# Two attention decodes on one core: the last 64 rows of A's wq moved in two 32-partition transfers

## The chip, the cores and the metric

The kernel runs on one core of one Trainium2 chip. The metric is the device time of one execution in microseconds. Before the change the median of three runs is 248.11 us (248.06 to 248.28).

## The reference

Two independent decode steps, A and B, each project one token, attend over a cache and project back. The outputs of both stand side by side. All arrays are bfloat16.

```python
# shapes of both: x [1,1,576], k_cache and v_cache [1,16,8192,128], wq [576,4096], wo [4096,576]
# 32 query heads of 128, 16 key/value heads, two query heads on each
q = (x @ wq).reshape(B, Sq, Hq, Dh)
k, v = ...            # A: the last W = 2048 positions of the cache; B: all 8192
scores = einsum(q, k) * Dh ** -0.5
o = einsum(softmax(scores), v)
out = o.reshape(B, Sq, Hq * Dh) @ wo
...
concatenate([a, b], axis=-1)   # [1,1,1152]
```

With one token the work is nearly all reading: per side 4.5 MB of wq and 4.5 MB of wo, for A 16 MB of cache, for B 64 MB, 102.8 MB in all.

## The kernel before

Every engine has a list of operations, written in program order by `op` and `load` (class `Prog`, L37 to L109); a wait is put ahead of an operation for each name in its `deps`. SP issues all big loads, one after another; ACT issues the two small loads of x.

**The ring.** All big loads go into one SBUF buffer, `ring`, of 73728 bfloat16 columns on 128 partitions. `place` (L181) takes the next stretch of columns (going back to the beginning where the rest is too short), lets the load wait for the last use of whatever lay there, and appends it to SP's list. The order of loads is: A's wq, B's wq, then K0, K1, V0, K2, V1, ... over twelve units (four of A with four key heads each, eight of B with two), then A's wo in one piece and B's wo in six pieces of 16, 8, 4, 2, 1 and 1 blocks of 576 columns.

**wq.** The 576 rows of a wq are loaded in two transfers. The main one (L212) puts rows 0 to 511 on 128 partitions, four consecutive rows on each. The tail (L214) takes the last 64 rows; each row of 4096 columns is cut into two halves, so that 64 rows become 128 partitions of 2048 columns: row r has its first half on partition 2r and its second on 2r + 1.

**The query projection.** The x row is spread over partitions by PE: `xT` (L282) multiplies pieces of x by a row of ones, which gives x values as columns, each repeated 128 times; DVE copies them into `xrep`. For the tail, `xdup` (L273) holds each of the last 64 values twice, and two copies with a mask (L288) make one version that is zero on odd partitions and one that is zero on even ones, so that the product with the halves of a row picks the right half. Then `qmm` (L323) makes, for each side, eight groups of 512 columns, with five matmuls each: four with main rows and one with the tail. A `qmm` waits for both wq transfers of its side. Its result goes to `ktb` and from there into `za` (A) and `zb` (B), the stationary operands of the scores.

**Attention.** Per unit, DVE transposes each slab of K (`T`, L367), PE makes the scores (`S`, L384), then come the maximum, the exponential (ACT, L433), another DVE transpose and the products with V (L460), accumulated and folded into one column per head (L476). The loads of later units wait for the `T` and `V` operations that use the ring's stretch before them; the first V loads wait for `qmm0.7` and `qmm1.7`.

**The end.** After the last unit the heads are normalised and multiplied by wo (`F`, L543), first A's piece, then B's six as they land; the 1x576 results of each side are copied to `outsb` (L551, L554) and stored (L555).

Of the kernel before, what the change touches and what calls it, by code (L numbers as in the profile page):

```python
# [14 lines left out]
DM = 576  # L15
# [21 lines left out]
class Prog:  # L37
# [9 lines left out]
    def op(self, eng, fn, deps=(), name=None):  # L47
        self.ops[eng].append((fn, tuple(deps), name, None))
        if name is not None:
            assert name not in self.where, name  # L50
            self.where[name] = (eng, len(self.ops[eng]) - 1)

    def load(self, eng, fn, sem, value, deps=(), name=None):
        self.ops[eng].append((fn, tuple(deps), None, sem))
        if name is not None:
            assert name not in self.dma, name
            self.dma[name] = (sem, value)
# [54 lines left out]
def bass_concat_heads__sliding_block_cached__gqa_block_cached__decode_kernel(nc, A_x, A_k_cache, A_v_cache, A_wq, A_wo,  # L112
                         B_x, B_k_cache, B_v_cache, B_wq, B_wo, out):
    xs, ks, vs = [A_x, B_x], [A_k_cache, B_k_cache], [A_v_cache, B_v_cache]
    wqs, wos = [A_wq, B_wq], [A_wo, B_wo]
# [10 lines left out]
    onesb = nc.alloc_sbuf_tensor("onesb", [1, 128], BF16)  # L126
    xrow = nc.alloc_sbuf_tensor("xrow", [1, 2 * DM], BF16)
    xdup = nc.alloc_sbuf_tensor("xdup", [1, 2, 128], BF16)
    xrep = nc.alloc_sbuf_tensor("xrep", [128, 2, 6, 128], BF16)
# [39 lines left out]
    def view(t, free, offset, dims, parts=128, p0=0):  # L169
        return bass.AP(tensor=t, offset=p0 * free + offset, ap=[[free, parts], *dims])  # L170

    pg = Prog(nc)
    op, load = pg.op, pg.load
    s_x = [nc.alloc_semaphore("s_x%d" % i) for i in range(2)]
    s_ld = [nc.alloc_semaphore("s_ld%d" % i) for i in range(NSEM)]
    s_out = nc.alloc_semaphore("s_out")


# [2 lines left out]
    def place(size, uses, issue, name):  # L181
        if at[0] + size > RING:
            at[0] = 0
        lo, hi = at[0], at[0] + size
        at[0] = hi
        deps = []
        for r in list(live):
            if r[0] < hi and lo < r[1]:
                deps += r[2]
                live.remove(r)  # L190
        n = nload[0]
        nload[0] += 1
        if n >= NSEM:
            deps += uses_of[n - NSEM]
        uses_of.append(list(uses))
        live.append((lo, hi, list(uses)))
        t = ring[:, lo:hi]
        load("sp", lambda e: issue(e, t), s_ld[n % NSEM], 16 * (n // NSEM + 1), deps=deps, name=name)
        return t

    for P in range(2):
        x = xs[P]
# [4 lines left out]
    wq_at = {}  # L207
    w = HQ * DH
    for P in range(2):
        uses = ["qmm%d.7" % P]  # L210
        main = wqs[P][0:512, :].rearrange("(p k) n -> p (k n)", k=4)
        wq_at[P, 0] = place(4 * w, uses, lambda e, t, main=main: e.dma_start(t, main), "wq%d.0" % P)  # L212
        tail = wqs[P][512:DM, :].rearrange("r (c n) -> (r c) n", c=2)
        wq_at[P, 1] = place(w // 2, uses, lambda e, t, tail=tail: e.dma_start(t, tail), "wq%d.1" % P)  # L214


    kv_at = {}
# [17 lines left out]
    for i in range(NU + 1):  # L235
        for kind, n in (("K", i), ("V", i - 1)):
            if 0 <= n < NU:
                side, u = UNITS[n]
# [11 lines left out]
    def slab(kind, side, u, s):  # L250
# [7 lines left out]
       deps=["id0"], name="ident")  # L258
# [7 lines left out]
    for c in range(2):  # L266
        op("dve", lambda e, c=c: e.tensor_reduce(par[:, c:c + 1], view(identf, 128, c, [[2, 64]]), AX.X, ALU.add),
           deps=["identf"], name="par%d" % c)


    banks = [sb[0], sb[1], qb[0], qb[1]]
    for P in range(2):
        op("dve", lambda e, P=P: e.tensor_copy(  # L273
            view(xdup, 256, 128 * P, [[2, 64], [1, 2]], parts=1),
            view(xrow, 2 * DM, P * DM + 512, [[1, 64], [0, 2]], parts=1)), deps=["x%d" % P], name="xd%d" % P)
        for k in range(5):
            def mm(e, P=P, k=k):
                if k < 4:
                    lhsT = view(xrow, 2 * DM, P * DM + k, [[4, 128]], parts=1)
                else:  # L280
                    lhsT = xdup[0:1, P, :]
                return e.matmul(banks[2 * P + k // 4][:, (k % 4) * 128:(k % 4 + 1) * 128], lhsT=lhsT,  # L282
                                rhs=onesb[0:1, :], start=True, stop=True)
            op("pe", mm, deps=["x%d" % P, "onesb", "xd%d" % P], name="xT%d.%d" % (P, k))
        op("dve", lambda e, P=P: e.tensor_copy(
            xrep[:, P, 0:4, :].rearrange("p k m -> p (k m)"), banks[2 * P][:, :]), deps=["xT%d.3" % P], name="xr%d.0" % P)
        for c in range(2):
            op("dve", lambda e, P=P, c=c: e.tensor_scalar(  # L288
                xrep[:, P, 4 + c, :], banks[2 * P + 1][:, 0:128], par[:, c:c + 1], None, ALU.mult),
                deps=["xT%d.4" % P, "par%d" % c], name="xr%d.%d" % (P, 1 + c))  # L290
# [5 lines left out]
    for h in range(2):  # L296
        op("dve", lambda e, h=h: e.tensor_reduce(
            cls[:, 2 * h:2 * h + 2], view(identf, 128, 64 * h, [[1, 2], [32, 2], [2, NB]]), AX.XY, ALU.add),
            deps=["identf"], name="clsB%d" % h)
    op("dve", lambda e: e.tensor_reduce(clsa[:], view(identf, 128, 0, [[1, 8], [8, 16]]), AX.X, ALU.add),  # L300
       deps=["identf"], name="clsa")
    op("dve", lambda e: e.tensor_reduce(sel[:], view(identf, 128, 0, [[1, 32], [32, 4]]), AX.X, ALU.add),
       deps=["identf"], name="sel")
    op("dve", lambda e: e.tensor_copy(mkr[:], view(ident, 128, 0, [[0, 128], [1, 4]], 4)),
       deps=["ident"], name="mkr")
    op("dve", lambda e: e.tensor_scalar(mkl[:], view(ident, 128, 0, [[0, 16], [1, 4], [0, 2]], 4), -1.0, BIG,
                                        ALU.add, ALU.mult), deps=["ident"], name="mkl")

    XR = ["xr%d.%d" % (P, c) for P in range(2) for c in range(3)]

    KT = NKT * SLAB
    for P in range(2):
        for n in range(8):
            u = 8 * P + n
            bank = banks[u % 4]

            def mm(e, P=P, n=n, bank=bank):
                for k in range(5):
                    if k < 4:
                        lhsT, o = xrep[:, P, k, :], wq_at[P, 0][:, k * w + n * 512:k * w + (n + 1) * 512]  # L320
                    else:
                        lhsT, o = xrep[:, P, 4 + n // 4, :], wq_at[P, 1][:, (n % 4) * 512:(n % 4 + 1) * 512]
                    ins = e.matmul(bank[:, :], lhsT=lhsT, rhs=o, start=(k == 0), stop=(k == 4))  # L323
                return ins
            op("pe", mm, deps=["wq%d.0" % P, "wq%d.1" % P] + XR + (["qe%d" % (u - 4)] if u >= 4 else []),
               name="qmm%d.%d" % (P, n))
            deps = ["qmm%d.%d" % (P, n)] + (["qT%d" % (u - 2)] if u >= 2 else [])
            if n % 2 == 0:
                op("act", lambda e, n=n, bank=bank: e.activation(qsb[:, n % 2, :], bank[:, :], ACT.Copy),  # L329
                   deps=deps, name="qe%d" % u)  # L330
            else:
                op("dve", lambda e, n=n, bank=bank: e.tensor_copy(qsb[:, n % 2, :], bank[:, :]),
                   deps=deps, name="qe%d" % u)
            op("dve", lambda e, n=n: e.transpose(  # L334
                ktb[:, n * 512:(n + 1) * 512].bitcast(I32), qsb[:, n % 2, :].bitcast(I32)),
                deps=["qe%d" % u] + (["z0.%d" % i for i in range(4)] if P else []), name="qT%d" % u)
        srcs = [[512, NP], [64, 2], [1, 2], [128, 2]]
        for b in range(4):
            if P == 1:
                op("dve", lambda e, b=b: e.tensor_copy(  # L340
                    view(zb, NP * 4 * ZW, 32 * b + W0, [[4 * ZW, NP], [2 * ZW, 2], [ZW, 2], [1, 2]], 32, 32 * b),
                    view(ktb, KT, b // 2 * 256, srcs, 32, 32 * b)),
                    deps=["qT%d" % u for u in range(8, 16)] + ["zb0"], name="z1.%d" % b)
            else:
                op("dve", lambda e, b=b: e.tensor_copy(
                    view(za, NQ * 4 * ZA, ZA - 128 + 32 * b, [[4 * ZA, NQ], [2 * ZA, 2], [ZA, 2], [1, 8]], 32, 32 * b),
                    view(ktb, KT, 0, [[1024, NQ], [64, 2], [1, 2], [128, 8]], 32, 32 * b)),
                    deps=["qT%d" % u for u in range(8)] + ["za0"], name="z0.%d" % b)
# [135 lines left out]
    for i in range(NU):  # L484
        n = nslab[i + 1] if i + 1 < NU else 0
# [37 lines left out]
       deps=["lsel", "lselA", "nb%d" % last, "mr%d" % last], name="L")  # L523
# [3 lines left out]
        deps=["rl", "O%d" % last], name="on")  # L527
    op("dve", lambda e: e.transpose(oq[:].rearrange("p c k -> p (c k)"), on[:].rearrange("p c k -> p (c k)")),
       deps=["on"], name="oq")
# [6 lines left out]
    for P in range(2):  # L536
        k0 = 0
        for c, kk in enumerate(NWO[P]):
# [11 lines left out]
        r = 64 * P  # L550
        op("act", lambda e, r=r: e.activation(outsb[r:r + 1, :], fb[r:r + 1, 0:288], ACT.Copy),  # L551
           deps=[done], name="f%d.0" % P)
        r = 64 * P + 32
# [37 lines left out]
```

## Time and profile before

| | |
|---|---|
| median of the runs | 248.11 us |
| profiled execution, its time | 248.34 us |
| profiled execution, span of the core's instructions | 246.5 us |
| PE busy | 182.0 us (74%) |
| DVE busy | 146.0 us (59%) |
| ACT busy | 23.6 us (10%) |
| moved by DMA | 102.91 MB, mean 418 GB/s |
| granted TensorE clock, mean | 0.827 |

The span runs from the first instruction of the program to the last; the profiled execution's own time has 1.8 us around it. Times in the views are counted from the span's start. The page's first rows give the busy share of each engine in forty slices of 6.2 us, a digit for each; "DMA" there is the mean of the core's sixteen DMA engines. A DMA has three times: when the queue (SPq) issues it, when its packets run on the DMA engines, and when it lands, which is when the last of its increments reaches the semaphore. The chain that ended last follows the work back from the last instruction: at each step to what released it. The packet records of the trace list, for each packet, its start, its length, its size and its queue; the landing records list every increment of each transfer. Neither names the DMA engine; a packet is put to an engine by its start, 3 ns ahead of the end of the packet before it.

### The profile page before, as it was taken

The page shows a single profiled execution, that of the slowest core. Times are in us where ns is not written, and L with a number is a line of the kernel's source. Part 1 is how long each engine was busy: PE and PEld are TensorE (multiplying, and loading weights), DVE is VectorE, ACT ScalarE, POOL GpSimd, SP SyncE. Part 2 cuts the span into 40 slices and gives each one's busy share as a digit, 9 for nine tenths or more (in the row PEclk, how much of TensorE's full clock was granted, in tenths as well). Part 3 has the DMA queues.
Part 4 walks back from the last instruction along what each step waited for, and adds up shares of the span by engine and source line. Part 5 has one row for each costly group of instructions (what it writes and reads, how often), then busy time and mean ns, then how long its engine had stood idle before and what let it go on. Part 6 is the DMA issues. An engine that isn't in the chain of part 4 may idle for free.

```text
span 246.5 us, 2421 instructions
## 1 busy us (share of the span) xinstructions
PE 182.0 (74%) x1009; PEld 75.6 (31%) x1009; DVE 146.0 (59%) x224; ACT 23.6 (10%) x48; POOL 1.8 (1%) x12
## 2 busy tenths in 40 slices
PE   1169958778868599489769858949929949985694
PEld 0024423223332152152142233224205205231461
DVE  3466976786869569169349448547646836922200
ACT  2002210101201010010001001001001001001000
POOL 2000000000000000000000000000000000000000
PEclk9999997799999958957955976965985895796579
DMA  6999999999999999999999999999999999999992
GB/s 261 425 479 402 433 425 419 425 425 463 431 417 431 425 425 431 423 441 452 441 431 433 425 431 425 425 423 427 431 425 431 449 431 431 431 437 431 401 406 103
DMA packets 5062, 102.91 MB, mean 418 GB/s; under 512 B 566, under 2 KB 828, under 8 KB 1340
## 3 DMA queue, kind: packets, MB, share of 16 engines
q1 hardware_dynamic: 5048, 102.77, 97.6%
q8 instruction: 8, 0.13, 0.2%
q14 instruction: 2, 0.02, 0.0%
q10 hardware_dynamic: 4, 0.00, 0.0%
HBM read 102.76 MB, written 0.00 MB: 417 GB/s over the span
## 4 chain that ended last, share of the span: by engine, by line
DMA 56%; PE 20%; DVE 19%; issue 1%; SPq 1%; ACT 0%; DVEq 0%
DMA ring<-in_B_k_cache_dram 41%; DVE ktb L367 15%; DMA ring<-in_B_wo_dram 10%; DMA ring<-in_A_wq_dram 5%; PE sb L323 4%; PE sb L384 4%; PE qb L384 4%; PE qb L323 3%; PE ob L476 3%; DVE pts L445 2%; PE mb L424 1%; SPq L246 1%; DVE pta L441 0%; PE qb L376 0%; DVE nb L430 0%
## 5 line engine op out<-in xcount | busy, mean ns | idle before, releaser
L367 DVE STREAM_TRANSPOSE ktb<-ring 128x1024 int32<-128x1024 int32 x80 | 95.1, 1221 | 16.7 <-DMA ring<-in_B_k_cache_dram 15.8
L384 PE MATMUL sb<-ktb,zb 128*128 128x512 bf16 x256 | 84.4, 468 | 27.3 <-DVE ktb L367 27.3
L384 PEld LDWEIGHTS sb<-ktb,zb 128*128 128x128 bf16 x256 | 23.2, 109 | 77.6 <-DVE ktb L367 45.3
L460 PE MATMUL vb<-ring,pts 128*16 128x512 bf16 x256 | 20.6, 412 | 2.6 <-DVE pts L445 2.6
L384 PE MATMUL qb<-ktb,za 128*128 128x512 bf16 x64 | 19.1, 436 | 2.9 <-DVE ktb L367 2.9
L476 PEld LDWEIGHTS ob<-sel,xo 128*128 128x128 f32 x96 | 19.5, 285 | 4.9 <-issue 2.2
L399 DVE TENSOR_REDUCE mx<-sb 128x1 f32<-128x512 f32 x8 | 5.5, 692 | 21.9 <-PE sb L384 21.9
L476 PE MATMUL ob<-sel,xo 128*128 128x4 f32 (+1 forms) x96 | 17.7, 309 | 0.7 <-ACT xo L467 0.7
L467 ACT ACTIVATE xo<-vb 128x512 f32<-128x512 f32 x12 | 7.2, 597 | 89.2 <-PE vb L460 89.2
L323 PE MATMUL sb<-ring,xrep 128*128 128x512 bf16 x40 | 11.4, 441 | 5.3 <-DMA ring<-in_A_wq_dram 5.3
L430 DVE COPY nb<-mb 128x1 f32<-128x1 f32 x12 | 1.9, 159 | 21.1 <-PE mb L424 21.1
L433 ACT ACTIVATE psb<-sb,nb 128x512 bf16<-128x512 f32 x8 | 5.5, 687 | 65.3 <-DVE nb L430 65.3
L445 DVE STREAM_TRANSPOSE pts<-psb 64x512 bf16<-64x512 bf16 x16 | 11.0, 688 | 1.0 <-ACT psb L433 0.8
L543 PE MATMUL qb<-ring,oP 128*1 128x288 bf16 x128 | 10.3, 328 | 1.2 <-DMA ring<-in_B_wo_dram 0.6
L384 PEld LDWEIGHTS qb<-ktb,za 128*128 128x128 bf16 x64 | 5.7, 106 | 13.4 <-DVE ktb L367 6.4
L401 PE MATMUL mb<-identf,mx 128*1 128x128 f32 x24 | 4.6, 271 | 7.1 <-DVE mx L399 7.1
L334 DVE STREAM_TRANSPOSE ktb<-qsb 128x256 int32<-128x256 int32 x16 | 7.1, 446 | 4.4 <-ACT qsb L329 4.0
L323 PE MATMUL qb<-ring,xrep 128*128 128x512 bf16 x40 | 9.4, 381 | 0.0
L460 PEld LDWEIGHTS vb<-ring,pts 128*16 128x16 bf16 x256 | 4.1, 90 | 16.9 <-issue 15.6
L323 PEld LDWEIGHTS sb<-ring,xrep 128*128 128x128 bf16 x40 | 4.2, 109 | 11.6 <-issue 8.2
L543 PEld LDWEIGHTS qb<-ring,oP 128*1 128x1 bf16 x128 | 5.6, 94 | 5.8 <-DMA ring<-in_B_wo_dram 2.2
L554 DVE CAST outsb<-qb 1x288 bf16<-1x288 f32 x2 | 0.9, 458 | 10.8 <-PE qb L543 10.8
(73 smaller groups left out, 71.9 us busy)
## 6 DMA issues: line engine op xcount, KB each, us to landing
ring<-in_B_k_cache_dram SPq DMA_DIRECT2D x8, 4096.0 KB, 25.3
ring<-in_B_v_cache_dram SPq DMA_DIRECT2D x8, 4096.0 KB, 33.0
ring<-in_A_k_cache_dram SPq DMA_DIRECT2D x4, 2048.0 KB, 30.9
ring<-in_A_v_cache_dram SPq DMA_DIRECT2D x4, 2048.0 KB, 26.4
ring<-in_A_wo_dram SPq DMA_DIRECT2D x1, 4608.0 KB, 16.4
ring<-in_A_wq_dram SPq DMA_DIRECT2D x1, 4096.0 KB, 12.1
ring<-in_B_wq_dram SPq DMA_DIRECT2D x1, 4096.0 KB, 22.2
ring<-in_B_wo_dram SPq DMA_DIRECT2D x1, 2304.0 KB, 21.5
```

Of the source, the lines that this page charges most:

```text
L323: ins = e.matmul(bank[:, :], lhsT=lhsT, rhs=o, start=(k == 0), stop=(k == 4))
L334: op("dve", lambda e, n=n: e.transpose(ktb[:, n * 512:(n + 1) * 512].bitcast(I32), qsb[:, n % 2, :].bitcast(I32)), deps=["qe%d" % u] + ([" ...
L367: op("dve", lambda e: e.transpose(kt.bitcast(I32), src.bitcast(I32)), deps=["K%d" % i] + (["S%d" % (k - NKT)] if k >= NKT else Z), name="T ...
L384: ins = e.matmul(bank[:, :], lhsT=lhsT, rhs=view(ktb, KT, (k % NKT) * SLAB + 64 * c + v, [[128, 16], [2, 32]]), start=(side == "B" and s = ...
L399: op("dve", lambda e: e.tensor_reduce(mx[:, 0:1], sbank[i][:, :], AX.X, ALU.max), deps=["S%d" % (k0[i] + nslab[i] - 1)] + (["mT%d" % (i - ...
L401: op("pe", lambda e: e.matmul(mb[0:1, 0:128], lhsT=mx[:, 0:1], rhs=identf[:, :], start=True, stop=True), deps=["max%d" % i] + was, name="m ...
L433: op("act", lambda e: e.activation(psb[:, :], sbank[i][:, :], ACT.Exp, bias=nb[:, c:c + 1], scale=SCALE, accum_out=acc), deps=["nb%d" % i, ...
L445: op("dve", lambda e, h=h: e.transpose(view(pts, 1024, 2 * h, [[4, 16], [64, 16], [1, 2]], 64, 64 * h), psb[64 * h:64 * h + 64, :]), deps= ...
L460: ins = e.matmul(vbank[i][32 * j:32 * j + n, :], lhsT=lhsT, rhs=src[:, 512 * j:512 * j + 512], start=(s == 0), stop=(s == nslab[i] - 1))
L467: op("act", lambda e: e.activation(xo[:, c, :], vbank[i][:, :], ACT.Copy), deps=["V%d.%d" % (i, nslab[i] - 1)] + (["O%d" % (i - 1)] if i e ...
L476: ins = e.matmul(ob[:, at:at + w], lhsT=xo[:, c, 128 * t:128 * t + 128], rhs=sel[:, w * t:w * t + w], start=(t == 0), stop=(t == 3))
L543: ins = e.matmul(fb[r:r + 1, 0:288], lhsT=oP[:, P, k0 + k:k0 + k + 1], rhs=wo_at[P, c][:, k * DM + 288 * n:k * DM + 288 * n + 288], start= ...
```

## The change

Only side A's tail is moved in another way; side B keeps the old one. The 64 rows are loaded whole, 4096 columns on each of 64 partitions, in two transfers of 32 partitions. In each, the source is written with an outer dimension of eight (rows one apart), a middle one of four (rows eight apart) and the row itself, so partition 4a + b of a transfer holds its row a + 8b. The second transfer goes to partitions 32 to 63 of the same stretch of the ring and has a semaphore of its own, `s_wq`, for which A's `qmm` waits too.

The x values follow: `xdup` holds A's last 64 values once, in the permuted order, the fifth `xT` makes 64 columns, one plain copy takes the place of the two masked ones, and the fifth matmul of each of A's eight groups contracts 64 partitions with the full rows. The stretch of the ring for A's tail grows from 2048 to 4096 columns.

```diff
+    s_wq = nc.alloc_semaphore("s_wq")
...
-        tail = wqs[P][512:DM, :].rearrange("r (c n) -> (r c) n", c=2)
-        wq_at[P, 1] = place(w // 2, uses, lambda e, t, tail=tail: e.dma_start(t, tail), "wq%d.1" % P)
+        if P == 0:
+            for i in range(2):
+                tail = bass.AP(tensor=wqs[P].tensor, offset=wqs[P].offset + (512 + 32 * i) * w,
+                               ap=[[w, 8], [8 * w, 4], [1, w]])
+                if i == 0:
+                    wq_at[P, 1] = place(w, uses, lambda e, t, tail=tail: e.dma_start(t[0:32, :], tail), "wq%d.1" % P)
+                else:
+                    load("sp", lambda e, t=wq_at[P, 1], tail=tail: e.dma_start(t[32:64, :], tail), s_wq, 16,
+                         name="wq%d.2" % P)
+        else:
+            tail = wqs[P][512:DM, :].rearrange("r (c n) -> (r c) n", c=2)
+            wq_at[P, 1] = place(w // 2, uses, lambda e, t, tail=tail: e.dma_start(t, tail), "wq%d.1" % P)
...
     for P in range(2):
-        op("dve", lambda e, P=P: e.tensor_copy(
-            view(xdup, 256, 128 * P, [[2, 64], [1, 2]], parts=1),
-            view(xrow, 2 * DM, P * DM + 512, [[1, 64], [0, 2]], parts=1)), deps=["x%d" % P], name="xd%d" % P)
+        dst, order = (([[2, 64], [1, 2]], [[1, 64], [0, 2]]) if P else
+                      ([[32, 2], [4, 8], [1, 4]], [[32, 2], [1, 8], [8, 4]]))
...
+        if P == 0:
+            op("dve", lambda e: e.tensor_copy(xrep[0:64, 0, 4, :], banks[1][0:64, 0:128]), deps=["xT0.4"], name="xr0.1")
+            continue
...
+                    elif P == 0:
+                        lhsT, o = xrep[0:64, P, 4, :], wq_at[P, 1][0:64, n * 512:(n + 1) * 512]
...
-            op("pe", mm, deps=["wq%d.0" % P, "wq%d.1" % P] + XR + (["qe%d" % (u - 4)] if u >= 4 else []),
+            op("pe", mm, deps=["wq%d.0" % P, "wq%d.1" % P] + ([] if P else ["wq0.2"]) + XR + (["qe%d" % (u - 4)] if u >= 4 else []),
```

More of the change, by code (lines that the diff above doesn't have):

```diff
@@ L272, in bass_concat_heads__sliding_block_cached__gqa_block_cached__decode_kernel @@
     for P in range(2):
-        op("dve", lambda e, P=P: e.tensor_copy(
-            view(xdup, 256, 128 * P, [[2, 64], [1, 2]], parts=1),
-            view(xrow, 2 * DM, P * DM + 512, [[1, 64], [0, 2]], parts=1)), deps=["x%d" % P], name="xd%d" % P)
+        dst, order = (([[2, 64], [1, 2]], [[1, 64], [0, 2]]) if P else
+                      ([[32, 2], [4, 8], [1, 4]], [[32, 2], [1, 8], [8, 4]]))
+        op("dve", lambda e, P=P, dst=dst, order=order: e.tensor_copy(
+            view(xdup, 256, 128 * P, dst, parts=1), view(xrow, 2 * DM, P * DM + 512, order, parts=1)),
+            deps=["x%d" % P], name="xd%d" % P)
         for k in range(5):
@@ L280, in mm @@
                 else:
-                    lhsT = xdup[0:1, P, :]
-                return e.matmul(banks[2 * P + k // 4][:, (k % 4) * 128:(k % 4 + 1) * 128], lhsT=lhsT,
+                    lhsT = xdup[0:1, P, 0:128 if P else 64]
+                m = 128 if k < 4 or P else 64
+                return e.matmul(banks[2 * P + k // 4][0:m, (k % 4) * 128:(k % 4 + 1) * 128], lhsT=lhsT,
                                 rhs=onesb[0:1, :], start=True, stop=True)
-            op("pe", mm, deps=["x%d" % P, "onesb", "xd%d" % P], name="xT%d.%d" % (P, k))
+            op("pe", mm, deps=["x%d" % P, "onesb"] + ["xd%d" % P], name="xT%d.%d" % (P, k))
         op("dve", lambda e, P=P: e.tensor_copy(
             xrep[:, P, 0:4, :].rearrange("p k m -> p (k m)"), banks[2 * P][:, :]), deps=["xT%d.3" % P], name="xr%d.0" % P)
+        if P == 0:
+            op("dve", lambda e: e.tensor_copy(xrep[0:64, 0, 4, :], banks[1][0:64, 0:128]), deps=["xT0.4"], name="xr0.1")
+            continue
         for c in range(2):
@@ L307, in bass_concat_heads__sliding_block_cached__gqa_block_cached__decode_kernel @@
                                         ALU.add, ALU.mult), deps=["ident"], name="mkl")
-    XR = ["xr%d.%d" % (P, c) for P in range(2) for c in range(3)]
+    XR = ["xr0.0", "xr0.1", "xr1.0", "xr1.1", "xr1.2"]
     KT = NKT * SLAB
```

## The prediction

> **What bounds the kernel now.** I read the page first: the DMA row and the queues. A share of 97.6% means that the sixteen DMA engines work on SP's queue from start to end, and no compute engine comes near that (PE 74%, DVE 59%).
>
> ```profile
> span 246.5 us, 2421 instructions
> DMA  6999999999999999999999999999999999999992
> q1 hardware_dynamic: 5048, 102.77, 97.6%
> q8 instruction: 8, 0.13, 0.2%
> q14 instruction: 2, 0.02, 0.0%
> ```
>
> The two "instruction" queues carry no tensor data, but share the engines with q1. They matter below.
>
> Second, the chain that ended last, for the place where a microsecond of DMA is felt. These pieces (start, length, what) are its beginning, one step in the middle and its end:
>
> ```profile
> 1.19 12.93 DMA ring<-in_A_wq_dram
> 14.20 4.43 PE sb L323 x10
> ...
> 59.93 25.24 DMA ring<-in_B_k_cache_dram
> ...
> 98.58 25.45 DMA ring<-in_B_k_cache_dram
> ...
> 218.84 24.77 DMA ring<-in_B_wo_dram
> 243.62 0.04 issue
> 243.66 0.31 PE qb L543 x2
> ```
>
> B's K loads end at 85.17 and 124.03, and four loads of 4096 KB go by in these 38.9 us, 9.7 us each. A K load that lands 25.2 us after its issue therefore stood behind 25.2 - 9.7 = 15.5 us of older work. Whatever delays SP by less than that leaves the DMA engines busy. So the end is set by the bytes each engine carries, and the last transfer lands when its slowest engine is done.
>
> Third, the table by stretches for the last microseconds (the number before GB/s is the DMA share):
>
> ```profile
> 240.00:241.00 1.00, 0.65 (x12) 0.26 (x9) 0.00 (x0) 0.00 (x0) 0.00 (x0) 1.00 1.04 399
> 241.00:241.50 0.50, 0.50 (x12) 0.35 (x10) 0.00 (x0) 0.00 (x0) 0.00 (x0) 1.00 0.67 229
> 241.50:242.00 0.50, 0.44 (x8) 0.09 (x2) 0.00 (x0) 0.00 (x0) 0.00 (x0) 1.00 0.53 203
> 242.00:242.50 0.50, 0.30 (x6) 0.23 (x8) 0.00 (x0) 0.00 (x0) 0.00 (x0) 1.00 0.53 189
> 242.50:243.00 0.50, 0.43 (x8) 0.11 (x6) 0.00 (x0) 0.00 (x0) 0.00 (x0) 1.00 0.24 85
> ```
>
> The share drops to 0.53 and stays there for a microsecond: half the engines are finished while the other half still work. The trace's landing records (one increment per engine and transfer) say the same for the last wo transfer: eight increments at 241.34 to 241.77, seven at 243.06 to 243.24, one at 243.62. A's first wq load landed on all sixteen within 12.37 to 12.85. The engines start level and end 1.4 us apart. The packet records show why: each of the first seven q8 packets (16 KB, at 37 to 229 us) stops one engine's q1 packets for about 1.05 us and makes the next one 0.5 us longer, each time on another engine. The two q14 packets (8 KB, 40 and 168 us) both hit an eighth engine, which is the one at 243.62. The eighth q8 packet, at 241.0, reached an engine of the early group that had just finished, and cost nothing.
>
> **The change part by part.** *The A tail's bytes.* Now 128 packets of 4 KB, eight per engine at a pitch of 156 ns, and a 6 ns completion: 1.25 us on every engine. After it there are 64 rows of 8 KB in two transfers. How many engines serve them is the question. Here, transfers of 128 partitions land in sixteen increments, the output with two rows in two, the x load with one row in one. With eight outer entries in DRAM and 32 partitions in SBUF the bounds are eight and sixteen engines; I take eight, since the short cases followed their row count. A packet of 8 KB lies between rows: 4 KB has a pitch of 156 ns, 9 KB of 349 and 16 KB of 607, which gives 306 ns (between 4 and 16 KB) to 310 ns (between 4 and 9 KB). Eight engines then carry 8 x 306 + 12 = 2.46 us instead of 1.25, +1.21 us (+1.24 by the upper price); the other eight carry nothing, -1.25 us. With sixteen engines it is 4 x 306 + 12 = 1.24 us, no change.
>
> [...]
>
> *Which eight, and what is late next.* The loaded eight should contain the engines that served x (one) and the output (two). Followed through the packet records, both output engines are in the early group: the first output's packets went out on them right after their last wo packet, at 241.73 and 241.81. Of the other six loaded engines nothing is recorded. Fourteen engines are left, eight of them late; if the six had no relation to lateness the chance of missing all eight would be 1 in 3003. Only order can make the halves coincide, and then eight successive fetches on eight different engines would have to include one loaded engine (the eighth fetch hit an early one) and seven unloaded ones. So I expect a late engine among the loaded. Is it the latest? Its very first packet started 61 ns after that of x's engine, second of sixteen, which places it near x's; but the second output engine started tenth or later, so that is weak. I take it as loaded: 243.62 + 1.21 = 244.83 for the last landing. If only engines of the 243.24 group are loaded: 243.24 + 1.21 = 244.45, +0.83.
>
> *The tail's landing and the first projection.* The tail landed at 14.1; with 2.46 us behind wq it lands near 15.3, and the first L323 matmul moves from 14.20 to about 15.4. The PE and DVE chain behind it, up to the K issue at 59.9, moves with it, and so do the SP waits on PE at L224 and on DVE. Cover: the 15.5 us of queued loads. If that were gone it would cost 1.2 us once more.
>
> *One more issue on SP.* The L214 issues took 0.41 and 0.52 us. The B wq, K and V issues behind it move by that; the engines need B's wq only near 13 us and it is issued at 1.6. Nothing.
>
> *Small work for x.* Two TENSOR_SCALAR of 342 ns on xrep become one copy of half the rows, bounded by 0 and 0.34 us; xdup's copy (0.40 us) gets another order of the same 64 values written once instead of twice. The last of them ends at 4.6, ten microseconds before the matmuls. The fifth matmul of eight groups contracts 64 rows instead of 128: the mask matmul of L376 with 4 rows took 0.39 us, L323's with 128 rows 0.379, so the rows don't set it. Nothing.
>
> *The ring.* A's tail takes 4096 columns instead of 2048, so wq1 and the first loads sit 2048 further. From V1 on each load lies at the old place, and I worked through the overlaps: every load waits for the same earlier uses as before. Nothing.
>
> *Sum.* Everything but the bytes is covered; last landing +1.21 us. The chain after it (0.31 PE, 0.47 cast, output) stays. The profiled execution took 248.34 with a span of 246.5, so 249.55 for it; it stood 0.23 above the median of the runs, 248.11, which becomes 249.3.
>
> **The rivals.** *Faster: the late eight are exactly the relieved eight.* Then the late group lands at 243.62 - 1.25 = 242.37 and the early one at 241.77 + 1.21 = 242.98, 0.64 earlier than 243.62: 247.5. It decides if no loaded engine loses more than 0.64 us to fetches in the run. For it: exactly eight engines are late, both output engines are early, and the shift is about the size of the gap. Against it: the eighth fetch at 241.0 hit an early engine; were that loaded, it would have 1.2 us of work left and would end near 241.6 + 1.2 + 1.1 to 1.5 = 243.9 to 244.3, and the gain turns into +0.2 to +0.7.
>
> *No change: sixteen engines serve it.* -0.02 us, 248.1. For it: the SBUF side has 32 partitions; against it: the small transfers' counts.
>
> *Slower by more: the cover fails.* If the 1.2 us of the first projection reached the loads too, 250.5. Against it the 15.5 us; I give it under 2 in 100, inside the first case below.
>
> **How the numbers follow.** A loaded engine is late: 0.67, which gives 248.9 to 249.5 (+0.83 to +1.24, widened by the 0.2 us by which the runs spread); its likeliest member is 249.3. Exact halves: 0.21, 247.4 to 247.7. Sixteen engines, or a delayed early engine that eats the gain: 0.12, 247.9 to 248.5. The slower and the faster case are both needed for 8 in 10, so the range runs from 247.4 to 249.6; the likeliest case alone has 248.9 to 249.6. A measurement of this kernel can tell about 0.2%, 0.5 us, from no change: the first case is slower beyond that, the second faster, the third within it, save that 0.01 of the last is slower: faster 0.21, same 0.11, slower 0.68.
>
> **What would show it.** Packets on q1: 5048 - 128 + 64 = 4984 if eight engines serve the tail, 5000 if sixteen (16 completions more). PE's idle before L323 on in_A_wq: 5.3 now, 6.5 after. The share in the last stretches: where it was 0.53 for a microsecond it should fall below that by steps, with a few engines working to about 244.5. If instead all engines end within half a microsecond and the last wo lands before 243.0, the halves coincided and my forecast has the wrong sign. If the K loads' time from issue to landing falls below 10 us, the cover failed.

## The result, and the profile after

The changed kernel takes 249.56 us (median of six runs, 249.48 to 249.71) against 248.19 us (six runs, 248.06 to 248.28): a ratio of 1.0051, interval 1.0041 to 1.0061, 1.37 us slower. The forecast was 249.3. The profiled execution took 249.55 us with a span of 247.7, 1.2 us more than before.

The page of the changed kernel, the rows that stand for the work of the DMA engines:

```profile
span 247.7 us, 2422 instructions
DMA  7998999999999999999999999999999999999991
q1 hardware_dynamic: 4984, 102.77, 97.2%
q8 instruction: 8, 0.13, 0.2%
q14 instruction: 2, 0.02, 0.0%
```

4984 packets on q1 are the count for eight engines (sixteen would make 5000), and the landing records agree: each of the two transfers of the tail lands in eight increments, the first at 13.71 to 14.02, the second at 14.95 to 15.26. The packet records show the two halves directly: eight engines start on B's wq at 12.36 to 12.71, the eight that serve the tail at 14.56 to 14.90. The eight that serve the tail are called the loaded ones below, the other eight the relieved ones. B's wq then lands in two groups, at 22.39 to 22.73 and at 24.69 to 25.00, where before it was one group from 23.4 to 23.8.

The chain that ended last, changed kernel (start, length, what):

```profile
2.10 13.16 DMA ring<-in_A_wq_dram
15.26 0.24 issue
15.50 4.76 PE sb L343 x10
...
220.04 24.82 DMA ring<-in_B_wo_dram
244.86 0.04 issue
244.90 0.31 PE qb L563 x2
```

The last landing moved from 243.62 to 244.86, by 1.24 us. What follows it is as long as before. The table by stretches, changed kernel (columns: length, busy time and instructions of PE, PEld, DVE, ACT and POOL, the granted clock, the DMA share, GB/s):

```profile
241.50:242.00 0.50, 0.00 (x0) 0.00 (x0) 0.00 (x0) 0.00 (x0) 0.00 (x0) 1.00 0.58 214
242.00:242.50 0.50, 0.43 (x8) 0.33 (x10) 0.00 (x0) 0.00 (x0) 0.00 (x0) 1.00 0.48 177
242.50:243.00 0.50, 0.50 (x12) 0.28 (x8) 0.00 (x0) 0.00 (x0) 0.00 (x0) 1.00 0.21 83
243.00:243.50 0.50, 0.27 (x6) 0.06 (x4) 0.00 (x0) 0.00 (x0) 0.00 (x0) 1.00 0.20 74
243.50:244.00 0.50, 0.50 (x8) 0.21 (x8) 0.00 (x0) 0.00 (x0) 0.00 (x0) 1.00 0.13 46
244.00:244.50 0.50, 0.44 (x6) 0.09 (x4) 0.00 (x0) 0.00 (x0) 0.00 (x0) 1.00 0.05 18
```

Before, half the engines stopped at one moment and the other half at another. Now most stop between 242 and 243, and the share of 0.20, 0.13, 0.05 is three engines, then two, then one of sixteen. The landing records of the last wo transfer, all sixteen engines, put side by side (in the changed kernel the two halves are told apart by the groups in which the loads before it landed):

```
before   241.34 241.56 241.58 241.63 241.63 241.65 241.70 241.77 | 243.06 243.07 243.09 243.10 243.14 243.19 243.24 | 243.62
after    241.66 241.71 241.79 241.91 241.94 241.99 242.22 243.12   (the eight that did not serve the tail)
         242.68 242.69 242.75 242.77 242.88 | 244.13 244.31 | 244.86   (the eight that did)
```

Of the eight that served the tail five were early, two belonged to the middle group and one was the very last.

### The profile page after: what moved, and what is told of

Same layout as the page of the kernel before. It is cut to its first block, busy times and chain, and to the rows that moved or that the text cites. A ratio compares the mean times of both kernels' runs of the same rounds, so it can differ in the third digit from the quotient of the medians.

```text
span 247.7 us, 2422 instructions
## 1 busy us (share of the span) xinstructions
PE 179.8 (73%) x1009; PEld 73.2 (30%) x1009; DVE 145.5 (59%) x223; ACT 23.6 (10%) x48; POOL 1.8 (1%) x12
## 3 DMA queue, kind: packets, MB, share of 16 engines
q1 hardware_dynamic: 4984, 102.77, 97.2%
## 4 chain that ended last, share of the span: by engine, by line
DMA 56%; PE 20%; DVE 19%; SPq 2%; issue 2%; ACT 0%; DVEq 0%
DMA ring<-in_B_k_cache_dram 31%; DVE ktb L387 15%; DMA ring<-in_B_wo_dram 10%; DMA ring<-in_B_v_cache_dram 10%; DMA ring<-in_A_wq_dram 5%; PE sb L343 5%; PE qb L404 4%; PE qb L343 4%; PE sb L404 3%; PE ob L496 2%; DVE pts L465 2%; PE mb L444 1%; SPq L258 1%; DVE pta L461 1%; PE qb L396 1%
## 5 line engine op out<-in xcount | busy, mean ns | idle before, releaser
L404 PE MATMUL sb<-ktb,zb 128*128 128x512 bf16 x256 | 80.7, 451 | 27.7 <-DVE ktb L387 27.7
L404 PEld LDWEIGHTS sb<-ktb,zb 128*128 128x128 bf16 x256 | 22.6, 106 | 75.7 <-DVE ktb L387 45.3
L496 PEld LDWEIGHTS ob<-sel,xo 128*128 128x128 f32 x96 | 18.6, 273 | 4.7 <-issue 1.9
L496 PE MATMUL ob<-sel,xo 128*128 128x4 f32 (+1 forms) x96 | 16.9, 301 | 0.7 <-ACT xo L487 0.7
L343 PE MATMUL sb<-ring,xrep 128*128 128x512 bf16 (+1 forms) x40 | 12.1, 441 | 6.6 <-DMA ring<-in_A_wq_dram 6.6
L343 PE MATMUL qb<-ring,xrep 128*128 128x512 bf16 (+1 forms) x40 | 10.6, 402 | 0.0
L343 PEld LDWEIGHTS sb<-ring,xrep 128*128 128x128 bf16 (+1 forms) x40 | 3.8, 104 | 14.2 <-issue 11.3
```

Source lines behind the costliest of these rows:

```text
L404: ins = e.matmul(bank[:, :], lhsT=lhsT, rhs=view(ktb, KT, (k % NKT) * SLAB + 64 * c + v, [[128, 16], [2, 32]]), start=(side == "B" and s = ...
L496: ins = e.matmul(ob[:, at:at + w], lhsT=xo[:, c, 128 * t:128 * t + 128], rhs=sel[:, w * t:w * t + w], start=(t == 0), stop=(t == 3))
```

## The experiments

All times are medians beside runs of the kernel before on the same chip (248.2 to 248.3 us in each set).

**The same two transfers on sixteen engines**

```diff
-                               ap=[[w, 8], [8 * w, 4], [1, w]])
+                               ap=[[w, 16], [16 * w, 2], [1, w]])
...
-                      ([[32, 2], [4, 8], [1, 4]], [[32, 2], [1, 8], [8, 4]]))
+                      ([[32, 2], [2, 16], [1, 2]], [[32, 2], [1, 16], [16, 2]]))
```

> The changed kernel with the outer dimension sixteen in place of eight (rows and x values permuted to match); all else as changed: two transfers, 64 full rows, the same waits. Theory 1, the bytes on each engine: sixteen engines carry two rows of 8 KB per transfer, 4 x 306 + 12 = 1.24 us each, as before the change (1.25), so 248.2 us, and the tail lands on sixteen engines near 14.1. Rival 2, the 1.2 us by which the first projection starts later, or the second transfer and its wait, cost the time: the projection's start goes back to 14.2 here, but transfer, wait and layout stay; if these were the cost, 249.5. Rival 3, sixteen engines writing to 32 partitions get in each other's way: the tail then lands near 15.3 on all sixteen, every engine is 1.2 us later to the end, 249.4.

Measured: 249.85 us, ratio 1.0070 (1.0057 to 1.0082). Theory 1 failed and rival 3 held, with a price a little higher than its 249.4. From the page of this kernel, and from its chain:

```profile
q1 hardware_dynamic: 5000, 102.77, 97.6%
```

```profile
219.94 25.01 DMA ring<-in_B_wo_dram
```

5000 packets: sixteen engines served the tail, two rows per transfer each. But half of the 8 KB packets took 573 ns or more (309 to 652) where all take 309 in the changed kernel, the tail landed on all sixteen at 14.96 to 15.94, and the last wo transfer landed at 244.96. The bytes per engine were those of before and the time was not: with sixteen engines writing to 32 partitions at a time a packet took up to 652 ns where it takes 309 with eight. What slows them there is not in the trace. So it would be wrong to say of the change that it is slow because only eight engines serve the tail; the 64 partitions cost 2.5 us of a loaded engine in either form. Rival 2 can't be judged here, as the projection started at 16.18 and not at 14.2; the run on B's tail below judges it.

**Partitions 64 to 127**

```diff
-                    wq_at[P, 1] = place(w, uses, lambda e, t, tail=tail: e.dma_start(t[0:32, :], tail), "wq%d.1" % P)
+                    wq_at[P, 1] = place(w, uses, lambda e, t, tail=tail: e.dma_start(t[64:96, :], tail), "wq%d.1" % P)
...            # the second transfer likewise from t[32:64, :] to t[96:128, :], and xT and its copy
-                        lhsT, o = xrep[0:64, P, 4, :], wq_at[P, 1][0:64, n * 512:(n + 1) * 512]
+                        lhsT, o = xrep[64:128, P, 4, :], wq_at[P, 1][64:128, n * 512:(n + 1) * 512]
```

> The changed kernel with A's tail on partitions 64 to 127 in place of 0 to 63, x values likewise; the outer dimension stays eight. With the outer dimension sixteen the 8 KB packets took 573 ns in the middle instead of 309, so two engines that write to the same few partitions share something. If what counts is only how many engines write to a transfer's partitions: eight engines, 309 ns, 249.5 us as the changed kernel. If partitions 64 to 127 are served by the same inlets as the eight other engines use for their half of B's wq at that time: packets near 600 ns, the loaded engines end their tail near 17 to 18 instead of 15.3, and the time goes up to 250.5 to 252.

Measured: 252.06 us, ratio 1.0149 (1.0135 to 1.0163). The 8 KB packets took 309 ns at best and 632 in the middle, and the loaded engines ended the tail at 17.59 to 18.15. The stretches from 12 to 16 us, first this kernel, then the changed one:

```profile
12.00:14.00 2.00, 0.00 (x0) 0.00 (x0) 1.95 (x2) 0.00 (x0) 0.00 (x0) 1.00 1.01 258
14.00:16.00 2.00, 0.00 (x0) 0.00 (x0) 1.67 (x8) 0.00 (x0) 0.00 (x0) 1.00 1.18 246
```

```profile
12.00:14.00 2.00, 0.00 (x0) 0.00 (x0) 1.94 (x2) 0.00 (x0) 0.00 (x0) 1.00 1.09 463
14.00:16.00 2.00, 0.50 (x2) 0.26 (x3) 1.74 (x8) 0.00 (x0) 0.00 (x0) 1.00 1.06 455
```

The share is full in both, but 250 GB/s flow instead of 460, and both halves are slow: the 32 KB packets that the relieved engines moved meanwhile took 1861 to 2504 ns, where every one of them takes 1213 in the changed kernel. So the two halves got in each other's way with the tail on partitions 64 to 127 (632 ns in the middle, 1861 to 2504) and not with it on 0 to 63 (309, 1213). That the relieved engines write their part of B's wq to partitions 64 to 127 would explain it; this is the author's guess, the trace doesn't name the partitions that an engine writes to. The two kernels differ in the partitions of the tail and of its x values alone, so the place of the tail decided between 309 and 632 ns.

**The edit on B's tail instead**

```diff
-        if P == 0:
+        if P == 1:
             for i in range(2):
...            # xdup, xT, xrep, qmm and the wait on wq1.2 likewise for P == 1
```

> The same edit with the outer dimension of eight, but on side B's tail; A's tail as before the change. Theory 1: the same eight engines carry 1.21 us more and the other eight 1.25 less, no matter which load it is, so the same time as the changed kernel, 249.5 us, while A's projection starts at 14.2 again. Rival 2, the later start of the first projection is what costs the time: 248.2, as B's projection waits for PE anyway.

Measured: 249.24 us, ratio 1.0045 (1.0033 to 1.0058); the last landing is 244.94. PE's idle time until A's wq is there, in this run and then in the changed kernel:

```profile
  DMA ring<-in_A_wq_dram: 5.0, 1
```

```profile
  DMA ring<-in_A_wq_dram: 6.6, 1
```

It was 5.3 before, and the projection starts at 14.2 again, as before. The time is that of the changed kernel within the intervals. So the later start of the projection is not what costs.

**Nothing but an extra load, on eight, four and two engines**

```diff
+        if P == 1:
+            extra = bass.AP(tensor=wqs[0].tensor, offset=wqs[0].offset, ap=[[w, 8], [8 * w, 4], [1, w]])
+            load("sp", lambda e: e.dma_start(ring[0:32, RING - w:RING], extra), s_xt, 16, name="extra")
```

The other two have 4 and 2 for 8, and 16 and 8 partitions for 32.

> The kernel before the change with one extra load behind A's tail: 32 rows of wq (256 KB) once more, into 4096 columns of the ring that nothing uses, written with an outer dimension of eight; nothing waits for it but the program's end. Theory 1: eight engines carry four packets of 8 KB more, 4 x 306 + 6 = 1.23 us, the other eight nothing more or less; if the engine that lands last is among the loaded, the last landing moves from 243.6 to 244.85 and the time to 249.4 us. This also says whether the relief of the other eight in the change was worth anything: the same time as the changed kernel would mean nothing. If only engines of the 243.24 group are among the loaded: 249.0. Rival, the loaded engines are all early: 243.0 on them, 248.2.

> The extra load again, now 16 rows (128 KB) with an outer dimension of four: 1.23 us more on four engines. The extra load of two engines cost nothing, that of eight 1.3 us, so the late engine that decides is one of the six between. If it is among the first four: 249.4 us. If only a late engine of the 243.24 group is: 243.24 + 1.23 = 244.47, 249.0. If the first four are all early: 243.0 on them, 248.2.

> As the extra load of eight, but 8 rows (64 KB) with an outer dimension of two, so 1.23 us more on two engines only. Theory 1 and the packet records: the output's two engines belong to the early group and these are the same two, 241.8 + 1.23 = 243.0, still ahead of the last engine at 243.6: no change, 248.2 us, though each of the two carries as much more as in the extra load of eight. Rival, any engine that gets 1.2 us more moves the end: 249.4.

Measured: eight engines 249.50 us, 1.0053 (1.0041 to 1.0066); four 249.45, 1.0049 (1.0036 to 1.0063); two 248.32, 1.0005 (0.9996 to 1.0014). The chain's last load, in this order:

```profile
220.01 24.76 DMA ring<-in_B_wo_dram
```

```profile
219.60 25.00 DMA ring<-in_B_wo_dram
```

```profile
218.69 25.02 DMA ring<-in_B_wo_dram
```

The ends are 244.77, 244.60 and 243.71. Each loaded engine carried the same four packets of 309 ns more. With two nothing happens: the two loaded engines land within the middle group, which had seven members and now has nine, at 242.83 to 243.35, ahead of the last one. With four nearly the whole price is there, 1.17 us by the medians and 0.98 in the landing. So the engine that decides is one of the four and none of the two. And with eight, where the other engines got no relief, the time equals that of the changed kernel: the 1.25 us taken off the eight others bought nothing.

The middle group is not made of the same engines in every kernel. With the extra load on eight, one loaded engine besides the last was late (244.37); in the changed kernel two were (244.13 and 244.31). The last engine was among the loaded both times.

**Four engines, and less for the rest**

```diff
+            tail = wqs[P][512:560, :].rearrange("r (c n) -> (r c) n", c=2)      # 96 partitions
...
+            for c in range(2):
+                rest = bass.AP(tensor=wqs[P].tensor, offset=wqs[P].offset + 560 * w + c * (w // 2),
+                               ap=[[w, 4], [4 * w, 4], [1, w // 2]])
+                load("sp", lambda e, t=wq_at[P, 1], rest=rest, c=c: e.dma_start(t[96 + c:128:2, :], rest), s_wq,
+                     16 * (c + 1), name="wq0.%d" % (2 + c))
```

> A smaller shift: of A's tail 48 rows move as before (96 partitions of 4 KB on sixteen engines), the last 16 rows in two transfers with an outer dimension of four, in halves of 4 KB on partitions 96 to 127. The first four engines carry 6 x 156 + 6 + 8 x 156 + 12 = 2.20 us instead of 1.25, +0.95; the other twelve 0.94, -0.31. If the first four engines are all early: they end near 242.7 and the last one at 243.3 instead of 243.6, 247.9 us, a little faster than before. If the deciding late engine is among the four: 244.57, 249.15. If only a 243.24 engine is: 244.2, 248.8.

Measured: 250.67 us, ratio 1.0099 (1.0085 to 1.0114), last landing 245.80. The sign is that of "the deciding engine is among the four", but the landing is 1.2 us later than the 244.57 expected for it, so the forecast of this run missed. The 4 KB packets, all 159 ns in the kernels before and after the change, took up to 296 here, and the four engines' last rows landed at 16.23 to 16.62. The other twelve, which carry less than before, were late too: the twelve foremost increments of B's main wq load came at 24.53 to 25.17, where all sixteen had come by 23.84 before the change. So all engines were slowed, and this run doesn't price four engines. It may be the same clash on few partitions as in the two experiments above; how much each part adds was not separated.

**Where the last engine's lag comes from**

```diff
+        for _ in range(16 if i < 8 else 0):
+            op("dve", lambda e: e.nop())
         op("dve", lambda e: e.tensor_reduce(mx[:, 0:1], sbank[i][:, :], AX.X, ALU.max),
```

> The kernel before the change with 128 instructions on DVE that do nothing, 16 ahead of the maximum of each of units 0 to 7, where DVE waits for PE. Theory: the 8 KB packets on q14 fetch DVE's instructions, 128 of them at a time, and always through the same DMA engine, the last to land; a third one inside the span delays that engine by another 0.9 us, so the last landing moves from 243.6 to about 244.5 and the time to 249.1, though no compute engine is late. Rival, the packets belong to something else or the extra one falls on an early engine: 248.2 to 248.4.

Measured: 248.25 us, ratio 0.9998 (0.9990 to 1.0007), with the same 2421 instructions in the trace and q14 packets at 39.84 and 167.90 as before. The nops left no instruction, so this run tells nothing of the theory; it was repeated with instructions that do something.

```diff
+    pad = nc.alloc_sbuf_tensor("pad", [1, 128], F32)
...
+        for j in range(16 if i < 8 else 0):
+            op("dve", lambda e, j=16 * i + j: e.memset(pad[:, j:j + 1], 0.0))
```

> The kernel before the change with 128 more DVE instructions, memsets of one element of a small tile of their own, 16 ahead of the maximum of each of units 0 to 7 (the 128 nops of the earlier run left no instruction in the trace and the q14 packets where they were). Theory: the 8 KB packets on q14 are DVE's next 128 instructions; with 128 more the second comes well ahead of 168 us and a third one falls inside the span, on the same DMA engine, the last to land: last landing 243.6 + 0.9 = 244.5, time 249.1, while DVE stays far from busy. If the third packet falls on another engine of the late or early group, or the packets are not DVE's, 248.2 to 248.4. If DVE's longer chain at the head of each unit costs the time itself, the last landing stays at 243.6 and the wait of PE for DVE grows.

Measured: 249.21 us, ratio 1.0037 (1.0024 to 1.0049). From the page of this kernel, and from its chain:

```profile
PE 179.8 (73%) x1008; PEld 75.2 (30%) x1009; DVE 147.7 (60%) x352; ACT 23.6 (10%) x48; POOL 1.8 (1%) x12
q14 instruction: 3, 0.02, 0.0%
```

```profile
219.37 25.01 DMA ring<-in_B_wo_dram
```

128 more DVE instructions bring a third q14 packet, at 86.35 us between those at 40.29 and 167.44, and the last landing is 244.38, 0.76 later. Of the other fifteen engines eight land by 241.83, six at 242.94 to 243.22 and one at 243.61. That one is not the engine of the q14 packets: it was 0.36 us behind the fifteen others at the first load already (13.18 against 12.82 at most). The landing records of the loads in between show where the third packet went. Behind the first engine to land, the last columns of each row, all sixteen sorted:

```
load landed from   83.24   1.16  1.85        2.27   (after the q14 packet at 40.29)
                   92.96         1.84  2.12  2.28   (after the one at 86.35)
                  160.94   1.74  1.78  1.85  2.13  2.30
                  170.65   1.74  1.77  1.85  1.91  2.31  3.08   (after the one at 167.44)
```

The engine at 1.16 goes to 2.12 and then to 3.08, and the others stay, save for those that 16 KB packets on q8 delay in between. Each q14 packet thus costs its engine 0.96 us, and all three fall on the same one. The end moved by 0.76 only, as this engine stood at 1.16 after its first packet and at 1.34 in the kernel before. DVE's 1.7 us of extra work is not the cause: all sixteen engines carry part of each load of the ring, and fourteen of them end where they did (eight by 241.83 and six by 243.22, before eight by 241.77 and seven by 243.24). Between the first two packets the trace has 128 DVE instructions, between the second and the third 121, and in the kernel before 121 between the two. So the count of q14 packets goes with that of DVE's instructions, with 121 to 128 of them between two packets. The records of the changed kernel and of the extra loads on two and on four engines show the same: the engine that the first q14 packet delays is the one that the second delays, by 0.96 to 1.03 us. That the packets carry these instructions is the author's reading of the counts and of the page's name for the queue, "instruction"; the trace doesn't show what a packet holds.

**Both tails**

```diff
-        if P == 0:
+        if True:
             for i in range(2):
...            # everything that follows likewise for both sides, a semaphore for each
```

> The changed kernel with the same edit on B's tail too. Theory: the eight engines carry 2 x 1.21 = 2.42 us more, 243.6 + 2.4 = 246.0 for the last landing, 250.6 us, and the eight others run ahead by 2.5 us more without any use. The ring moves by another 2048 columns, and B's first K load no longer waits for a transpose of unit 0, which gives SP more lead. Rival, the cover fails, as the loads land 2.4 us later and SP waits for what is made of them: more than 250.9. Rival, the engines even out with time: less than 250.2.

Measured: 250.47 us, ratio 1.0091 (1.0075 to 1.0106); last landing 245.75, 2.13 us later than before the change against 2.42 expected. The early engines of the loaded eight are 2.2 to 2.4 us later too (243.87 to 244.16 where the changed kernel has 242.68 to 242.88 and the kernel before 241.6). The price is nearly that of two tails; the cover did not fail. The last engine is 0.3 us short of the sum. In the landing records the first q14 packet leaves it 1.01 us behind the foremost of the loaded engines here and 1.28 in the changed kernel, and the second adds about 1.0 in both. So the 0.3 us is how far ahead it stood among the loaded by then; why it stood there is open.

## Why the prediction was right

*What bounds the kernel.* As forecast: the end follows the most loaded engine. The extra loads show it without any other change: 1.23 us on two engines that have 1.8 us to spare cost nothing, the same on four or eight that include the last one cost 1.2 to 1.3.

*The bytes.* The price of an 8 KB packet was taken as 306 ns of pitch between those of 4 and 16 KB; the packets took 309 with 3 ns of overlap. Eight engines was the right end of the bounds. Forecast last landing 244.83, measured 244.86. By time the price was 1.37 us by the medians against the 1.2 forecast, 249.56 against 249.3.

*Which engines.* The argument was that eight engines chosen without regard to lateness hardly miss eight late ones, and that the two of the output, known as early, are among them. Both hold. Three of the eight were late. That the loaded eight contain the engines of x and of the output was taken as given in the prediction; the packet records of the changed kernel show it: the first output's packets start at 242.249 and 242.339, right behind the last wo packets of two engines that landed among 242.68 to 242.88, the early ones of the loaded eight. The engine of x starts on x at 1.645 and on wq at 1.783, and its eight packets of 8 KB run from 12.350 to 14.806. The two-engine load was free. That the latest is among them rested on a weak sign, its first packet being second of sixteen. The trace doesn't secure even that sign: at places two packets start within 1 ns of each other (37.352 and 37.353 us), and a packet is put to an engine by its start alone. The four-engine load confirms that the latest engine is among the loaded, which the sign would not have earned; here the prediction was lucky.

*The rival of a gain* needed the late and the relieved eight to be the same. Five of the relieved were late, three were not, and the relief was worth nothing in any case while the last engine was loaded. As the middle group differs from kernel to kernel, the late engines of the kernel before are no sure guide to those of the changed one.

*The rival of no change* had the sixteen-engine form at 248.1. Had the transfer been served by sixteen engines, the time would not have been 248.1 but 249.85: the rival was priced by bytes per engine alone and lacked the term of the partitions written to, 573 ns or more instead of 309 for half of the packets. The prediction's number did not rest on it, but its account of the change did: "how many engines serve them is the question" is half of it, where they write is the other. It is luck, too, that a wrong answer to that question would have done no harm: with sixteen engines the kernel would have been slower by about as much.

*The cover.* L343 starts 1.3 us later, at 15.50 where 15.4 was forecast, and the first K transpose 3.0 us later (39.66 against 36.62), since PE took longer for the projection. Here the prediction has a term wrong. It put the matmul that contracts 64 rows at nothing, from the duration of one with 4 rows. Two groups of A's projection, ten matmuls of which two contract 64 rows in the changed kernel, first before and then after the change:

```profile
20.82 2.16 PE sb L323 x10
22.98 2.16 PE qb L323 x10
```

```profile
23.54 2.58 PE sb L343 x10
26.12 2.58 PE qb L343 x10
```

That is 0.21 us more for each group of five; with B's tail in place of A's, ten matmuls of B's groups take 2.58 to 2.63 us. Why is not shown. A's eight groups took 13.2 us instead of 10.9. It cost nothing: in the run with an extra load on two engines the first K transpose is 1.25 us later than before (37.87) at no price, and with both tails it is 4.4 us later (41.01) while the kernel pays no more than the bytes. The statement that SP's lead of 15.5 us keeps all engines busy to the end is wrong for the last stage, though. The wo load is issued only at 217.1, when the last K is transposed, and the four foremost of the relieved engines had landed all of V by 218.2 to 218.3. The stretch after the issue, before and after the change:

```profile
217.00:218.00 1.00, 1.00 (x12) 0.25 (x10) 0.00 (x0) 0.00 (x0) 0.00 (x0) 1.00 0.91 393
```

```profile
217.00:218.00 1.00, 1.00 (x12) 0.30 (x4) 0.04 (x1) 0.00 (x0) 0.00 (x0) 1.00 0.69 295
```

There they ran dry: before, all sixteen engines have a packet under way throughout; after, twelve do at 218.0 and fourteen up to 219.0. The relieved engines gave back their lead: the four foremost were 2.4 us ahead of the loaded early ones at the V load (218.18 to 218.34 against 220.59 to 220.78) and 0.8 to 1.4 at the next (230.34 to 230.72 against 231.51 to 231.70). It cost nothing because the last engine was loaded all the time, but a gain that depended on lead at the end would have been lost here.

## What to carry to other kernels

In a kernel bound by DMA, look at the sixteen landing times of the last transfers, not at the mean share: a mean of 97% hid a spread of 2.3 us, and what counts is the bytes on the last engine. Here the extra load with an outer dimension of eight was paid by the eight engines that carried it, at 1.2 us for 32 KB per engine (four packets of 309 ns), and the tail that sixteen engines wrote to 32 partitions at a time by all sixteen (half of its packets at 573 ns or more). Beside the wide stream only the load on two engines known to be early was free (248.32 us against 248.2). And to find which engine decides, add the same small load on two, four and eight engines.

## What the runs showed of the hardware that was not expected

- The 8 KB packets of q14, a queue whose kind the page calls "instruction", all hit one DMA engine, which lands last of sixteen (243.62 before the change, 244.38 with the memsets). Each costs it 0.96 us in the run with the memsets. There 128 memsets of one element brought one packet more and cost 0.9 us of kernel time (249.21 against 248.32), with DVE busy for 60%.
- Packets of 8 KB that took 309 ns from eight engines on partitions 0 to 63 took 573 ns or more, half of them, from sixteen engines (32 partitions at a time), and 632 in the middle from eight engines on partitions 64 to 127 beside B's wq. The DMA share stayed full: in the second case 258 and 246 GB/s at a share of 1.01 and 1.18, where the changed kernel has 463 and 455 at 1.09 and 1.06. The share counted the slowed packets as busy.
- A group of five matmuls in which one contracts 64 rows and four contract 128 took 1.29 us, with all five at 128 rows 1.08.
